# The first batch's attention: eight scalings of the second head on GpSimd, those of the last pair on ScalarE, and four copies of k on VectorE

## The chip, the cores and the metric

The kernel runs on one core of a Trainium2 chip. The metric is the device time of one execution in microseconds. A core has five engines that run their own instruction streams and meet through semaphores: TensorE (PE; its weight loads are PEld), VectorE (DVE), ScalarE (ACT), GpSimd (POOL) and SyncE (SP), which issues nearly all transfers here.

## The reference

The input is q, k and v in 4 batches of 8 heads, 768 positions of 64 channels. Attention with a window of 96 positions and 8 global ones and a linear distance bias is followed by a mixture of four two-layer networks over its output.

```python
scores = scale * np.matmul(q, k.transpose(0, 1, 3, 2)) + bias
scores = np.where(keep, scores, -1000000000.0)
a = np.exp(scores - np.max(scores, axis=-1, keepdims=True))
a = a / (np.sum(a, axis=-1, keepdims=True) + 1e-09)
x = np.matmul(a, v)
...
for e in range(E):
    h = np.maximum(x @ w1[e], 0.0)
    out += p[:, e:e + 1] * (h @ w2[e])
```

## The kernel before

The four batches' attention and networks share one program. Only the first batch's attention stands alone, at the start (`attention_early`); the other three run in small steps between the matmuls of the networks (`attention_chain`). All arithmetic here is in f32, and the networks' products in f32r parts.

**Tiles and steps.** The early attention goes over four pairs of heads, in the order `PAIRS = (0, 2, 1, 3)`; m is the place in that order, so the last pair is m = 3. Each pair has six tiles of 128 positions (t). I number a tile by n = 6m + t, 0 to 23, and the step that takes it up by the same number; two or three steps without a new tile follow. One call of `flow` is a step, and there four tiles are under way:

- the scores of tiles n and n+1 are multiplied on TensorE when n is even (`scores_early`, tile `ps`);
- in `softmax`, tile n-1 gets for each of its two heads j bias, sum and row minimum on VectorE (the `CUSTOM_DVE_ANT_0` rows) and the exponential with its row sum on ScalarE (`ACTIVATE pb<-pb,nmax` and a read of the accumulator);
- in the same call tile n-2 gets 1e-9 added to its sums (`zsum`), their reciprocal, and the scaling of its probabilities `pb` by it, head 0 and then head 1. All of that is on VectorE; the scalings are the rows `TENSOR_SCALAR_CACHE_REDUCE pb<-pb,zsum`;
- in `turn`, tile n-3 is transposed by TensorE into `pt` (the rows `pt<-ident,pb`, four transposes, each of which needs the scaled half that it turns), and ScalarE copies it to `pT`;
- once three tiles are turned, `weigh` multiplies them with v (`px`), and ScalarE copies that to `x`.

A tile with t = 0 has half as many columns.

**Preparing the next pair.** `AHEAD` says behind which steps a piece of `prepare_early` is called: q's first three tiles, k's first, k's second, q's second. TensorE transposes three tiles of 128x128 into a `pt` tile and ScalarE copies or scales them into `early_q` or `early_k` (128x384). Behind k's first half GpSimd spreads the global columns (`COPY early_k<-early_k`); ahead of k's second half `windows` starts a transfer `vg<-v` and a copy of it on GpSimd. Those of the pair m = 1 are at the steps 3 to 6 (k's halves at 4 and 5), of m = 2 at 7 to 10 (k's at 8 and 9), of m = 3 at 12 to 15 (k's at 13 and 14).

**GpSimd's other work in this part.** `biases` makes the distance biases of two heads at a time (`nbias`, two instructions of 128x384) behind the steps 3, 6 and 8. At the end of step 9 `load_plain(2)` starts the transfer of the network's first weights into `w1s`, and `load_w2` the next; at the end of step 11 GpSimd gets the four sums over those weights (`TENSOR_TENSOR w1s<-w1s`). From step 14 it splits `w2s`, from step 19 it makes the next unit's sums and `w1s`. VectorE gets four sums of the attention's output (`xB`, `first_sums(0)`) behind the steps 17 to 20.

**Order.** The wrapper `Ordered` is on through all of this: each instruction is tied behind the one written before it on its engine, so each engine's order is that of the program, and so is SyncE's order of transfers. Waits are for data and for free buffers: the transfer of v for m = 3, ahead of `w1s` in SyncE's queue, needs the buffer that m = 0's v leaves once tiles 3 to 5 are weighed.

Of the kernel before, what the change touches and what calls it, by code (L numbers as in the profile page):

```python
# [18 lines left out]
P = 128  # L19
# [167 lines left out]
def attn_moe_kernel(ctx: ExitStack, tc, q, k, v, n_global, n_local, domain_probs, w1, w2, out):  # L187
# [5 lines left out]
    NPAIR = H // 2  # L193
# [16 lines left out]
    ve, ac, po, sy, te = (Ordered(tc, e) for e in (nc.vector, nc.scalar, nc.gpsimd, nc.sync, nc.tensor))  # L210

    PAIRS = (0, 2, 1, 3)
# [2 lines left out]

    BIASES = ((0, 1), (0, 3), (1, 0), (1, 2))

    ONSTEPS = 6

    HELDSTEPS = 14  # L220
# [108 lines left out]
    def transpose_half(A, nat, hf):  # L329
        tp = A.pt.tile([P, 512], F32, name="pt")  # L330
        for t in range(TPH):
            te.transpose(tp[:, t * P : (t + 1) * P], nat[:, hf * TPH + t].rearrange("p j d -> p (j d)"), ident)
        return tp
# [30 lines left out]
        if hf == 0:  # L364
            ve.tensor_copy(kd[:, :, :, P:], f32(kd[:, :, 0:1, :NGLOB]).to_broadcast([P, 2, NQT, NGLOB]))

    def prepare_early(A, nat, hf, name, got):

        tp = transpose_half(A, nat, hf)
        tpv = tp[:, :HALF].rearrange("p (t c) -> p t c", c=P)  # L370
        pl = slice(hf * TPH, (hf + 1) * TPH)
        if name == "q":
            if hf == 0:
                got["q"] = A.qd.tile([P, NQT, P], F32, name="early_q")
            ac.activation(got["q"][:, pl, :], tpv, AF.Copy, scale=-SCALE)
            return
        if hf == 0:
            got["k"] = A.kd.tile([P, NQT, PL], F32, name="early_k")
        dst = got["k"]
        ac.copy(dst[:, pl, :P], tpv)  # L380
        if hf == 0:
            po.tensor_copy(dst[:, :, P:], dst[:, 0:1, :NGLOB].to_broadcast([P, NQT, NGLOB]))

    def windows(A, vt):

        vg = A.vg.tile([P, 2, NQT, D], F32, name="vg")
        sy.dma_start(vg[:NPREV], vt[NGLOB:])
        po.tensor_copy(vg[NPREV:], vt[:NGLOB, :, 0:1, :].to_broadcast([NGLOB, 2, NQT, D]))
        return vg
# [17 lines left out]
    def scores_early(A, t0, got):  # L407


        heads = [A.ps.tile([P, 2, 2 * P], F32, name=f"ps{j}") for j in range(2)]  # L410
        for t in (t0, t0 + 1):
            c0 = max(t - 1, 0) * PL + (0 if t == 0 else NGLOB)
            n = P if t == 0 else 2 * P
            for j in range(2):
                own = slice(j * D, (j + 1) * D)
                win = got["k"].rearrange("p t c -> p (t c)")[own, c0 : c0 + n]
                te.matmul(heads[j][:, t - t0, :n], got["q"][own, t, :], win, start=True, stop=True)
        return [[heads[j][:, i] for j in range(2)] for i in range(2)]

    def softmax(A, new, old):  # L420


        if old:
            pb, zsum = old["pb"], old["zsum"]
        if new:
            t, pr, ps = new["t"], new["pr"], new["ps"]
            cols = slice(0, P) if t == 0 else slice(0, 2 * P)
            bcol = slice(2 * P, 3 * P) if t == 0 else slice(0, 2 * P)
            new["pcol"] = pcol = slice(P, 2 * P) if t == 0 else slice(0, 2 * P)
            nmax = A.small.tile([P, 2], F32, name="nmax")  # L430
            new["zsum"] = A.small.tile([P, 2], F32, name="zsum")
            new["pb"] = A.pb.tile([P, 2, 2 * P], F32, name="pb")
        for j in range(2):
            if new:
                e = new["pb"][:, j, pcol]
                ve.tensor_tensor_reduce(
                    e, ps[j][:, cols], nbias[:, 2 * pr + j, bcol], 1.0, 3.0e38, ALU.add, ALU.min, nmax[:, j : j + 1]
                )
                ac.activation(
                    e, e, AF.Exp, bias=nmax[:, j : j + 1], scale=-1.0, accum_out=new["zsum"][:, j : j + 1]  # L440
                )
            if old:
                if j == 1:
                    ve.reciprocal(zsum, zsum)
                elif A.early:

                    old["spare"] = spare = A.small.tile([P, 3], F32, name="spare")
                    ve.tensor_scalar(zsum, zsum, 1e-9, None, op0=ALU.add, op1=ALU.add, accum_out=spare[:, 2:3])
                else:
                    ac.activation(zsum, zsum, AF.Copy, bias=1e-9)  # L450
        if old:
            for j in range(2):
                p = pb[:, j, old["pcol"]]
                if A.early:
                    ve.tensor_scalar(
                        p, p, zsum[:, j : j + 1], None, op0=ALU.mult, op1=ALU.add, accum_out=old["spare"][:, j : j + 1]
                    )
                else:
                    ac.activation(p, p, AF.Copy, scale=zsum[:, j : j + 1])

    def turn(A, tile_):

        t, pb = tile_["t"], tile_["pb"]
        pt = A.pt.tile([P, 2, 2, P], F32, name="pt")
        pT = A.pT.tile([P, 2, 2, P], F32, name="pT")
        w0 = 1 if t == 0 else 0
        for w in range(w0, 2):
            for j in range(2):
                te.transpose(pt[:, w, j, :], pb[:, j, w * P : (w + 1) * P], ident)
        ac.copy(pT[:, w0:], pt[:, w0:])  # L470
        tile_["pT"] = pT
# [27 lines left out]
    def attention_early(A):  # L499

        b = 0
        x = xs[b] = xp.tile([P, NPAIR, S], F32, name="x")
        tiles, turned, ahead = [None] * 4, [], [None]

        def flow(new=None):

            one, two, three, four = tiles
            if new:
                if new["t"] % 2 == 0:
                    new["ps"], ahead[0] = scores_early(A, new["t"], gots[new["pr"]])  # L510
                else:
                    new["ps"] = ahead[0]
            if four:
                turned.append(four)
            softmax(A, one, two)
            if three:
                turn(A, three)
            if len(turned) == TPH:
                weigh(A, turned, x, b)
                turned.clear()  # L520
            tiles[:] = [new, one, two, three]

        def start(pr):

            nats[pr] = {n: next(load(A, src, b, pr, n)) for n, src in (("q", q), ("k", k), ("v", v))}

        def prepare_all(pr):

            nat, got = nats[pr], gots[pr]
            got["v"] = nat  # L530
            prepare_early(A, nat["q"], 0, "q", got)
            if pr:
                yield 1
            prepare_early(A, nat["k"], 0, "k", got)
            yield 1
            nat["vg"] = windows(A, nat["v"])
            prepare_early(A, nat["k"], 1, "k", got)
            yield 1
            prepare_early(A, nat["q"], 1, "q", got)
            yield 1  # L540

        nats, gots = {}, [{} for _ in range(NPAIR)]
        halves = [load(A, src, b, 0, n, 2) for n, src in (("q", q), ("k", k))]
        bias = biases(start_stack.enter_context(tc.tile_pool(name="setup", bufs=1)))
        next(bias)
        nats[0] = dict(zip(("q", "k"), (next(h) for h in halves)))
        for h in halves:
            next(h)
        nats[0]["v"] = next(load(A, v, b, 0, "v"))
        todo = [prepare_all(pr) for pr in PAIRS]  # L550
        next(bias)
        next(todo[0])
        start(PAIRS[1])
        for m, pr in enumerate(PAIRS):
            cur = gots[pr]
            for t in range(NQT):
                if t == 2 and m + 2 < NPAIR:
                    start(PAIRS[m + 2])
                flow({"t": t, "pr": pr, **cur})
                if (m, t) in BIASES:  # L560
                    next(bias)
                for _ in range(AHEAD[m][t]):
                    while todo and next(todo[0], 0) == 0:
                        todo.pop(0)
                yield
        while any(tiles):
            flow()
            yield
# [401 lines left out]
    with ExitStack() as start_stack:  # L970
        A = Pools(start_stack, "start", st=1, kd=2, qd=2, nat=2, natv=3, pb=4, ps=2, pt=3, px=1, early=True)
# [15 lines left out]
    A = Pools(  # L987
        att_stack, "att", st=1, kd=1, qd=2, nat=1, natv=1, pb=2, ps=2, pt=2, px=0, early=False, side="right"
    )
# [373 lines left out]
    for b in range(LATE):  # L1363
# [9 lines left out]
        for n, (fn, i) in enumerate(events):  # L1373
# [15 lines left out]
            for _ in fn(i):  # L1389
                work_chores()  # L1390
                done += 1
                if b == 0 and done == ONSTEPS:
                    next(mix, None)
# [59 lines left out]
```

## Time and profile before

| | us |
|---|---|
| median of 3 runs | 1162.91 (1162.72 to 1163.08) |
| span of the profiled execution | 1162.9 |
| early attention, in the span | from the start to about 60 |
| networks and the other attentions | about 60 to the end |

The profiled execution's own time is its span, 1162.9 us; nothing lies around it that the times show. TensorE is busy 98% of the span, VectorE 73%, ScalarE 53%, GpSimd 52%. Times of the trace are microseconds from the span's start. In a row, the first number is the start, the second the length; a bracket gives the idle time before it and what ended it. Lengths of successive instructions on one engine overlap a little, so the distance from start to start is what one costs. The line L43 is the wrapper `Ordered`, so rows are told apart by their tiles.

### The profile page before, as it was taken

The page shows a single profiled execution, that of the slowest core. Times are in us where ns is not written, and L with a number is a line of the kernel's source. Part 1 is how long each engine was busy: PE and PEld are TensorE (multiplying, and loading weights), DVE is VectorE, ACT ScalarE, POOL GpSimd, SP SyncE. Part 2 cuts the span into 40 slices and gives each one's busy share as a digit, 9 for nine tenths or more (in the row PEclk, how much of TensorE's full clock was granted, in tenths as well). Part 3 has the DMA queues.
Part 4 walks back from the last instruction along what each step waited for, and adds up shares of the span by engine and source line. Part 5 has one row for each costly group of instructions (what it writes and reads, how often), then busy time and mean ns, then how long its engine had stood idle before and what let it go on. Part 6 is the DMA issues. An engine that isn't in the chain of part 4 may idle for free.

```text
span 1162.9 us, 21146 instructions
## 1 busy us (share of the span) xinstructions
PE 1140.5 (98%) x7474; PEld 1062.6 (91%) x7474; DVE 853.2 (73%) x1944; ACT 618.2 (53%) x1597; POOL 606.6 (52%) x592
## 2 busy tenths in 40 slices
PE   7899999999999999999999999999999999999997
PEld 5678898989888989899998899999999999999997
DVE  7977776767767777776776777777777777777776
ACT  6854767777653665655565334444445444444443
POOL 5676645554343314222222327777778855555554
PEclk9999999999999999999999999999999999999999
DMA  9558798778775889978868668888887687777764
GB/s 185 149 172 290 268 294 258 269 253 255 247 261 206 282 269 286 282 234 279 257 196 288 207 215 304 306 302 300 284 314 281 240 303 239 249 247 247 245 232 131
DMA packets 181744, 294.32 MB, mean 253 GB/s; under 512 B 86400, under 2 KB 137088, under 8 KB 169344
## 3 DMA queue, kind: packets, MB, share of 16 engines
q1 hardware_dynamic: 177600, 286.61, 75.0%
q10 hardware_dynamic: 4032, 6.30, 1.5%
q8 instruction: 61, 1.00, 0.4%
q14 instruction: 51, 0.42, 0.1%
HBM read 207.93 MB, written 70.78 MB: 240 GB/s over the span
## 4 chain that ended last, share of the span: by engine, by line
PE 87%; DVE 5%; ACT 3%; POOL 2%; DMA 1%; issue 1%; DVEq 0%; ACTq 0%; POOLq 0%
PE pm L43 36%; PE pf L43 19%; PE X L43 11%; PE Y L43 9%; PE pt L43 7%; PE ps L43 4%; ACT pb L43 1%; DVE pb L43 1%; POOL w1s L43 1%; PE px L43 1%; DVE acc L43 1%; DVE xB L43 1%; DMA x_last<-piece 0%; DVE hA L43 0%; DVE pm L43 0%
## 5 line engine op out<-in xcount | busy, mean ns | idle before, releaser
L43 PE MATMUL pm<-w2s,h 128*128 128x512 f32 x1152 | 282.8, 395 | 3.6 <-DVE h L43 2.6
L43 PEld LDWEIGHTS pm<-w2s,h 128*128 128x128 f32 x1152 | 210.7, 188 | 46.5 <-DVE h L43 4.5
L43 ACT ACTIVATE hf<-pf 128x384 f32<-128x384 f32 x128 | 62.8, 491 | 248.3 <-DVE pf L43 247.1
L43 POOL TENSOR_TENSOR hS<-sf,hS 128x384 fp32r<-128x384 f32 x126 | 134.3, 1084 | 113.0 <-ACT hS L43 112.2
L43 DVE SCALAR_TENSOR_TENSOR acc<-pm,prob,acc 128x512 f32<-128x512 f32 x180 | 132.4, 748 | 54.5 <-PE pm L43 53.6
L43 POOL TENSOR_TENSOR sums<-raw 128x256 f32<-128x256 f32 x54 | 39.2, 745 | 211.8 <-DMA raw<-in_moe_w_dram 133.4
L43 PE MATMUL pm<-xT,w1s 128*128 128x384 f32 x744 | 147.9, 341 | 0.0
L43 PE MATMUL pf<-xT,w1s 128*128 128x384 f32 x768 | 146.5, 335 | 0.9 <-ACT hf L43 0.7
L43 PEld LDWEIGHTS pf<-xT,w1s 128*128 128x128 f32 x768 | 131.4, 188 | 1.7 <-ACT hf L43 1.2
L43 PEld LDWEIGHTS pm<-xT,w1s 128*128 128x128 f32 x744 | 128.0, 188 | 0.7 <-issue 0.7
L43 ACT ACTIVATE pb<-pb,nmax 128x256 f32<-128x256 f32 (+1 forms) x192 | 94.2, 498 | 58.1 <-DVE nmax L43 54.2
L43 DVE TENSOR_TENSOR hA<-hf,hA 128x384 fp32r<-128x384 f32 x94 | 84.6, 925 | 50.6 <-ACT hA L43 49.1
L43 PE MATMUL pm<-xB,w1s 128*128 128x384 f32 x574 | 116.8, 344 | 0.1
L43 PE MATMUL pf<-xB,w1s 128*128 128x384 f32 x576 | 110.7, 335 | 0.2 <-ACT hf L43 0.2
L43 PEld LDWEIGHTS pm<-xB,w1s 128*128 128x128 f32 x574 | 99.9, 188 | 5.5 <-issue 1.4
L43 ACT ACTIVATE h<-pm 128x384 fp32r<-128x384 f32 x128 | 62.0, 490 | 74.4 <-DVE pm L43 73.3
L43 PEld LDWEIGHTS pf<-xB,w1s 128*128 128x128 f32 x576 | 98.7, 188 | 0.6 <-ACT hf L43 0.4
L43 POOL TENSOR_TENSOR sf<-hf 128x384 f32<-128x384 f32 x63 | 70.3, 1116 | 43.6 <-ACT hf L43 43.6
L43 DVE CUSTOM_DVE_ANT_0 pb<-ps,nbias 128x256 f32<-128x256 f32 (+1 forms) x192 | 72.3, 395 | 5.8 <-PE ps L43 4.8
L43 DVE SCALAR_TENSOR_TENSOR h<-pm,h 128x384 fp32r<-128x384 f32 x128 | 69.5, 550 | 8.4 <-ACT h L43 6.8
L43 PE MATMUL Y<-w2b,hS 128*128 128x256 f32 x576 | 74.0, 282 | 0.0
L43 PE MATMUL X<-w2b,hS 128*128 128x256 f32 x576 | 73.9, 282 | 0.0
(159 smaller groups left out, 2183.5 us busy)
## 6 DMA issues: line engine op xcount, KB each, us to landing
w1s<-kept SPq DMA_DIRECT2D x47, 1792.0 KB, 8.2
w2b<-kept SPq DMA_DIRECT2D x224, 256.0 KB, 4.3
kept<-w1s SPq DMA_DIRECT2D x16, 1792.0 KB, 7.3
raw<-in_moe_w_dram SPq DMA_DIRECT2D x43, 512.0 KB, 4.7
kept<-w2s SPq DMA_DIRECT2D x16, 1024.0 KB, 6.9
w2s<-kept SPq DMA_DIRECT2D x16, 1024.0 KB, 5.5
qd<-qd SPq DMA_DIRECT2D x48, 192.0 KB, 3.2
v<-in_v_dram SPq DMA_DIRECT2D x16, 384.0 KB, 4.1
```

The source lines that it names most:

```text
L43: ins = fn(*args, **kwargs)
```

## The change

The second head's scaling (j = 1) leaves VectorE for 14 of the 24 tiles. Eight, listed in `BY_POOL` as (m, t), go to GpSimd as `tensor_scalar_mul`: the tiles 2, 4, 5, 7, 9, 10, 11 and 12. All six of the last pair fall to the `else` branch and become activations on ScalarE. The accumulator's read behind each of the 14 scalings goes with them. ScalarE's four copies into `early_k` of the pairs m = 1 and m = 2 become copies on VectorE, at the same place of the program. No transfer is added or moved.

```diff
+    BY_POOL = ((0, 2), (0, 4), (0, 5), (1, 1), (1, 3), (1, 4), (1, 5), (2, 0))
...
-    def prepare_early(A, nat, hf, name, got):
+    def prepare_early(A, nat, hf, name, got, pr):
...
-        ac.copy(dst[:, pl, :P], tpv)
+        (ve.tensor_copy if pr in PAIRS[1:3] else ac.copy)(dst[:, pl, :P], tpv)
...
-                if A.early:
+                if A.early and j == 1 and (old["m"], old["t"]) in BY_POOL:
+                    po.tensor_scalar_mul(p, p, zsum[:, j : j + 1])
+                elif A.early and (j == 0 or old["m"] < NPAIR - 1):
                     ve.tensor_scalar(
                         p, p, zsum[:, j : j + 1], None, op0=ALU.mult, op1=ALU.add, accum_out=old["spare"][:, j : j + 1]
                     )
...
-                flow({"t": t, "pr": pr, **cur})
+                flow({"t": t, "pr": pr, "m": m, **cur})
```

The four calls of `prepare_early` pass `pr` on.

## Rows read from the trace of the kernel before

**Rows 1.** Stretches: length, busy time of PE, PEld, DVE, ACT, POOL, clock, DMA.

```profile
20.00:40.00 20.00, 19.89 (x198) 15.38 (x198) 18.34 (x119) 20.00 (x69) 11.04 (x14) 1.00 0.67 168
60.00:74.00 14.00, 12.70 (x42) 7.62 (x42) 11.75 (x24) 6.78 (x11) 8.55 (x7) 1.00 0.28 81
74.00:110.00 36.00, 35.88 (x194) 33.45 (x195) 26.57 (x48) 16.83 (x35) 30.77 (x30) 1.00 0.87 296
```

**Rows 2.** Timeline of ScalarE: start, us, engine, operation, idle before.

```profile
17.34 0.59 ACT L43 COPY pT<-pt 128x512 f32<-128x512 f32 x1 [0.65 <-PE pt L43]
17.82 0.48 ACT L43 COPY early_k<-pt 128x384 f32<-128x384 f32 x1
18.20 0.52 ACT L43 ACTIVATE pb<-pb,nmax 128x256 f32<-128x256 f32 x1
...
18.70 0.50 ACT L43 ACTIVATE pb<-pb,nmax 128x256 f32<-128x256 f32 x1
...
33.94 0.68 ACT L43 COPY pT<-pt 128x512 f32<-128x512 f32 x1
...
43.03 0.51 ACT L43 ACTIVATE pb<-pb,nmax 128x256 f32<-128x256 f32 x1 [1.27 <-DVE zsum L43]
...
52.99 0.51 ACT L43 ACTIVATE pb<-pb,nmax 128x256 f32<-128x256 f32 x1 [0.20 <-DVE zsum L43]
```

**Rows 3.** Timeline of VectorE over one step, and the next one's start.

```profile
15.13 0.42 DVE L43 CUSTOM_DVE_ANT_0 pb<-ps,nbias 128x256 f32<-128x256 f32 x1
...
15.90 0.16 DVE L43 RECIPROCAL zsum<-zsum 128x2 f32<-128x2 f32 x1
16.09 0.48 DVE L43 TENSOR_SCALAR_CACHE_REDUCE pb<-pb,zsum 128x256 f32<-128x256 f32 x1
...
16.50 0.47 DVE L43 TENSOR_SCALAR_CACHE_REDUCE pb<-pb,zsum 128x256 f32<-128x256 f32 x1
...
16.90 0.42 DVE L43 CUSTOM_DVE_ANT_0 pb<-ps,nbias 128x256 f32<-128x256 f32 x1
```

**Rows 4.** Timeline of TensorE.

```profile
17.14 0.49 PE L43 MATMUL pt<-ident,k 128*128 128x128 f32 x3
...
23.54 0.66 PE L43 MATMUL pt<-ident,pb 128*128 128x128 f32 x4
...
25.87 0.39 PE L43 MATMUL px<-pT,v 128*64 128x128 f32 x4
...
32.53 0.60 PE L43 MATMUL pt<-ident,pb 128*128 128x128 f32 x4
```

**Rows 5.** Timeline of GpSimd.

```profile
19.68 4.78 POOL L43 TENSOR_SCALAR nbias<-dist 128x384 bf16<-128x384 f32 x4
...
34.16 2.92 POOL L43 TENSOR_TENSOR w1s<-w1s 128x256 f32<-128x256 f32 x4 [7.04 <-DMA w1s<-in_moe_w_dram]
37.03 0.34 POOL L43 COPY early_k<-early_k 128x192 f32<-128x192 f32 x1
...
40.91 1.27 POOL L43 TENSOR_TENSOR w2s<-raw,w2s 128x512 fp32r<-128x512 f32 x1
```

**Rows 6.** Timeline of SyncE's queue.

```profile
27.50 0.58 SPq L43 DMA_DIRECT2D w1s<-in_moe_w_dram  x1
```

**Rows 7.** Groups by line and form on GpSimd: xcount | busy, mean ns.

```profile
L43 POOL TENSOR_SCALAR nbias<-dist 128x384 bf16<-128x384 f32 x6 | 7.0, 1177 | 1.0 <-DVE dist L43 0.7
...
L43 POOL TENSOR_SCALAR low<-rel 128x256 f32<-128x256 f32 x1 | 1.1, 1098 | 0.1
...
L43 POOL CAST w1s<-raw 128x256 fp32r<-128x256 f32 x1 | 0.4, 391 | 0.0
```

**Rows 8.** The same view on VectorE, an operation with a PSUM input.

```profile
L43 DVE TENSOR_TENSOR pm<-pm,vv 128x384 f32<-128x384 f32 x64 | 35.7, 558 | 4.4 <-PE pm L43 4.3
```

**Rows 9.** Timeline of VectorE: two of the four sums of x.

```profile
41.28 1.31 DVE L43 TENSOR_TENSOR xB<-x 128x384 f32<-128x384 f32 x1
...
48.47 0.55 DVE L43 TENSOR_TENSOR xB<-x,xB 128x384 f32<-128x384 f32 x1
```

More of the change, by code (lines that the diff above doesn't have):

```diff
@@ L530, in prepare_all @@
             got["v"] = nat
-            prepare_early(A, nat["q"], 0, "q", got)
+            prepare_early(A, nat["q"], 0, "q", got, pr)
             if pr:
                 yield 1
-            prepare_early(A, nat["k"], 0, "k", got)
+            prepare_early(A, nat["k"], 0, "k", got, pr)
             yield 1
             nat["vg"] = windows(A, nat["v"])
-            prepare_early(A, nat["k"], 1, "k", got)
+            prepare_early(A, nat["k"], 1, "k", got, pr)
             yield 1
-            prepare_early(A, nat["q"], 1, "q", got)
+            prepare_early(A, nat["q"], 1, "q", got, pr)
             yield 1
```

## The prediction

> **What bounds the kernel now.** I read the stretches first. Behind the first attention TensorE has no room: from 74 to 110 us it works 35.88 of 36 us, from 60 to 74 it still misses 1.3 [rows 1]. Whatever moves the end of the first attention therefore moves the end of the kernel, and little can take it up again: at most that 1.3. So the question is only when the first attention ends, near 60 us.
>
> There the timelines of the engines count. From 20 to 40 us ScalarE is busy without a gap (20.00 of 20) while TensorE shows 19.89 and VectorE 18.34 [rows 1]; three engines are close together, so each can be what others wait for. In the last pair it is VectorE: ScalarE waits 1.27 us at 43.03 and 0.20 at 52.99, both ended by VectorE [rows 2]. A plain step costs VectorE 1.77 (15.13 to 16.90): the reciprocal starts 0.77 into it, head 0's scaling 0.96, head 1's 1.37, and a scaling costs 0.41 from start to start [rows 3].
>
> GpSimd looks free in sums of busy time, and it is not when it matters. At 19.68 it runs four bias instructions, 4.78 us. Then it stands 7.04 us for the weights in `w1s` and makes their four sums from 34.16 to 37.08; the spreading of k's global columns, written behind them, starts at 37.03 [rows 5]. The weights' transfer is issued at 27.50 [rows 6], and SyncE comes to it behind v's transfer, which needs the buffer left when tiles 3 to 5 are weighed, at 25.87 + 0.39 = 26.26 [rows 4].
>
> **The change part by part.**
>
> *Work removed.* VectorE loses 14 scalings: 8 to GpSimd (seven at 0.41, the half tile 12 less), 6 to ScalarE. ScalarE loses four copies at 0.38 (17.82 to 18.20), 1.5 in all [rows 2]. Taken alone this would be worth up to 1.5 us where ScalarE is full. It is the price of the waits that decides.
>
> *A copy of k on VectorE.* No such copy stands in the trace. The nearest row with a PSUM input of 128x384 is a sum, 558 ns [rows 8]; a scaling of 0.48 costs 0.41 from start to start [rows 3], so I take 0.5, between 0.41 (a scaling of fewer columns) and 0.56. The copy also waits: in step 4 VectorE would be free at 16.50, with head 1 gone to GpSimd, but TensorE's transposes of k run from 17.14 to 17.63 [rows 3, 4]. VectorE idles 1.1 us, copies to 18.13, and only then starts step 5, which began at 16.90. Queued behind the copy are the minima, so ScalarE's exponentials too. Step 5 has both scalings of tile 3 (1.77, to 19.90) and k's second copy (to 20.40). Step 6 starts there; tile 4's scaling is free for GpSimd at 20.40 + 0.96 = 21.36.
>
> *A scaling on GpSimd.* The trace has none of 128x256 by one operand per partition. A plain cast of that form takes 0.391, a two-operation one 1.098; the one-operation bias product takes 1.177 for 384 columns [rows 7], and two thirds of it are 0.79. I take 0.85, nearest to that row plus some start. [...]
>
> *First stall.* GpSimd takes tile 4 from 21.36 to 22.21. Next in its order stand the two bias products of step 6, half of the 4.78 [rows 5]: to 24.60. Only then tile 5: to 25.45. TensorE transposed tile 5 at 23.54 [rows 4]. It stands there 1.9 us later than before, and with it k's transposes of the pair m = 2, the weighing of tiles 3 to 5 and, through the buffer, the transfer of `w1s`. Bounds by the scaling's price: at 0.391 1.0 us late, at 1.098 2.4; nothing, if GpSimd gets tile 4 at the old time and is quick.
>
> *Second stall.* Tiles 10, 11 and 12 are written for steps 12 to 14, behind the four sums of step 11. Their start follows the weighing of tiles 3 to 5 by 34.16 - 26.26 = 7.90, nearly all of it transfer, and that distance stays, since the same transfers are issued in the same order from the same event. So the sums start at 26.26 + 1.9 + 7.9 = 36.1, end 2.92 later at 39.0, and tile 10 is scaled at 39.8. TensorE transposed tile 10 at 32.53 [rows 4, 5]. It stands there, 7.3 us behind, with the next pair's k and scores queued behind it. Tiles 11 and 12 then follow on GpSimd in 0.85 and less, ahead of TensorE. VectorE and ScalarE can run about a step ahead and stop.
>
> *What is given back.* ScalarE copied tile 10's transposes at 33.94, 0.8 after they ended at 32.53 + 0.60 [rows 2, 4]; TensorE's delay eats this slack first: 7.3 - 0.8 = 6.5 reach ScalarE. The first sum of x took 1.31 beside a GpSimd product that began at 40.91, another 0.55 [rows 5, 9]; late by 6 us, it meets GpSimd waiting for the next weights, and 0.75 come back. It might meet other work as before; then nothing does.
>
> *Last pair.* VectorE's step falls from 1.77 to 1.36. ScalarE's was two exponentials at 0.50 and a copy at 0.48 (17.34 to 17.82) [rows 2], 1.48; an activation of the same form adds at most 0.50 (an exponential's whole price) and at least 0.41 (VectorE's): 1.89 to 1.98, over VectorE's old 1.77. ScalarE takes the place of VectorE as the bound. In the first two such steps VectorE's earlier start (0.27 and 0.41) can be worth 0.7; the five full ones lose up to 5 x 0.21 = 1.0. I take 0.3 lost. That the engine relieved was the bound of this stretch gains nothing, since the work goes to the next in line.
>
> *The sum.* + 6.5 - 0.75 + 0.3 = 6.1 us later at the end of the attention. The measured execution's span, 1162.9, is the median's 1162.91; so 1169.0 us. Own range: the scaling at 0.391 takes 0.9 from the first stall and 0.5 from the second (1167.6), at 1.098 adds 0.75 (1169.8); no first stall at all leaves 1167.1; with the last pair's 0.7 gained, 1166.1; without the 0.75 and with 1.0 lost in the last pair on top of 1169.8, 1171.2. That is 1166.1 to 1171.2.
>
> **The rivals.**
>
> *GpSimd is in time, and it gets faster.* This needs the sums done before tile 10 is due: TensorE at 32.53, less 0.85 and 2.92, so weights landed by 28.8, 1.3 us after the issue that in the trace takes 6.7 to the sums [rows 4 to 6]. Or GpSimd would have to pass over waiting sums; the row at 37.03, which starts only when the last sum is through, speaks against it. If it held, ScalarE's 1.5 us of copies would be saved where it is full, and the 0.7 of the last pair's first steps: 1160.7.
> [...]
>
> *The stall is small.* The weights land sooner than they did, as TensorE's delay leaves the transfer queues emptier. If the sums do not wait at all, GpSimd gets to them when tile 9 is scaled, one step of VectorE (1.77) before tile 10 is due. Their 2.92 then leave 1.15, and the slower scaling 0.44 more. With the first stall that is 1.9 + 1.6 - 0.8 - 0.75 + 0.3 = 2.3: 1165.2. For it speaks that v, `vg`, two weights share the queues; against it that all four are still issued together.
>
> *The delay is taken up later.* The 1.3 us that TensorE misses from 60 to 74 and slack in the weights' splits would have to hold it; 6 us do not fit into that [rows 1]. If it were so, 1163.
>
> **How the numbers follow.** A difference of 0.2%, 2.3 us, is about what a measurement of this kernel can tell from none: 1160.6 to 1165.2. The forecast with both waits gets 0.70, the small stall 0.13 (at 1165.2 half of it within 0.2%), no visible change 0.08, the gain 0.09 (at 1160.7 half of it within 0.2%). So slower 0.70 + 0.06 = 0.76, same 0.07 + 0.08 + 0.04 = 0.19, faster 0.05. The likeliest case lies at 1166.1 to 1171.2; reaching into the small stall, 1164.6 to 1171.5 leaves out 2 in 10.
>
> **What would show it.** On GpSimd the first bias product of the second group starts behind a scaling, and tile 5's scaling behind two of them; four sums of `w1s` near 36 us, then two scalings in a row. On TensorE a wait of over 4 us ended by GpSimd ahead of one transpose group, near 35 to 40 us, and a shorter one near 24. On VectorE a wait for TensorE ahead of each of the four copies. In the last pair ScalarE without gaps. Attention ends near 66 instead of 60, and TensorE's stretches after it look as they did. The forecast is wrong if a scaling of tile 10 runs ahead of the sums, if the weights land well before 35, or if the GpSimd scaling costs over 1.1 us or under 0.4.

## The result and the profile after

The change makes the kernel slower: 1175.14 us in the median of 4 runs (1173.39 to 1176.82) beside 1162.99 (1162.72 to 1165.34) for the kernel before on the same chip. The ratio is 1.0096, with an interval of 1.0078 to 1.0114, which is 11.2 us of 1163; the two medians differ by 12.2. Two later measurements of the same kernel gave 1.0073 and 1.0083 (below); the mean of the three is 1.0084, 9.8 us. The forecast was 1169.0, with 1171.5 as its upper end: the sign held, the size was too small.

The profiled execution took 1176.82 us for a span of 1175.0. So 1.8 us lie outside the span here, and 1.7 to 1.9 in every later run that lists both. That the profiled execution of before took just its span, as told ahead of the prediction, is therefore doubtful. The forecast's difference of 6.1 doesn't depend on it.

The place of the loss is the one foreseen. ScalarE's last copy of the attention's output came at 59.98 before; after, the timeline of ScalarE has

```profile
41.32 0.59 ACT L43 COPY pT<-pt 128x512 f32<-128x512 f32 x1 [4.18 <-PE pt L43]
...
73.25 0.48 ACT L43 COPY x<-px 128x384 f32<-128x384 f32 x1 [0.89 <-PE px L43]
```

The first row answers to 33.94 in [rows 2]: tile 10's transposes are copied 7.4 us later, and the attention ends 13.3 later. The spans differ by 12.1, so all but 1.2 of it reaches the end. The question is the step from 7.4 to 13.3.

GpSimd's timeline after, beside [rows 5]:

```profile
21.82 0.92 POOL L43 TENSOR_SCALAR pb<-pb,zsum 128x256 f32<-128x256 f32 x1 [1.97 <-ACT pb L43]
22.71 2.40 POOL L43 TENSOR_SCALAR nbias<-dist 128x384 bf16<-128x384 f32 x2
25.21 0.92 POOL L43 TENSOR_SCALAR pb<-pb,zsum 128x256 f32<-128x256 f32 x1
26.10 2.30 POOL L43 TENSOR_SCALAR nbias<-dist 128x384 bf16<-128x384 f32 x2
...
36.49 2.89 POOL L43 TENSOR_TENSOR w1s<-w1s 128x256 f32<-128x256 f32 x4 [2.95 <-DMA w1s<-in_moe_w_dram]
39.36 1.82 POOL L43 TENSOR_SCALAR pb<-pb,zsum 128x256 f32<-128x256 f32 x2
```

Tile 4's scaling, two bias products, tile 5's scaling; later the four sums, and behind them the tiles 10 and 11 in one go. TensorE's timeline, beside [rows 4]:

```profile
24.66 0.33 PE L43 MATMUL pt<-ident,pb 128*128 128x128 f32 x1
26.19 0.55 PE L43 MATMUL pt<-ident,pb 128*128 128x128 f32 x3 [1.19 <-POOL pb L43]
...
35.69 0.27 PE L43 MATMUL pt<-ident,pb 128*128 128x128 f32 x1
40.33 0.90 PE L43 MATMUL pt<-ident,pb 128*128 128x128 f32 x3 [4.37 <-POOL pb L43]
41.02 0.85 PE L43 MATMUL pt<-ident,k 128*128 128x128 f32 x3
41.80 2.08 PE L43 MATMUL ps<-early_k,early_q 64*128 64x256 f32 x8
...
58.98 0.98 PE L43 MATMUL pt<-ident,pb 128*128 128x128 f32 x2 [2.17 <-DVE pb L43]
...
62.65 2.08 PE L43 MATMUL ps<-early_k,early_q 64*128 64x256 f32 x8
```

Both stalls stand where they were forecast, ended by GpSimd. What was not forecast stands behind them: three transposes of k take 0.85 instead of 0.49 [rows 4], and eight score products 2.08, where the same eight took 1.14 in the steps in between. The windows of the kernel after show the clock that goes with it (columns as in [rows 1]; the figure ahead of the DMA share, third from the end, is the granted clock):

```profile
36.00:38.00 2.00, 0.00 (x0) 0.00 (x0) 0.79 (x6) 1.15 (x5) 1.43 (x3) 0.96 0.07 28
38.00:44.00 6.00, 3.67 (x15) 2.52 (x16) 0.15 (x2) 2.05 (x6) 4.10 (x7) 0.50 0.01 3
44.00:46.00 2.00, 2.00 (x21) 1.83 (x22) 1.94 (x12) 1.04 (x3) 0.00 (x0) 0.83 0.00 0
58.00:60.00 2.00, 0.96 (x4) 0.47 (x6) 1.96 (x13) 1.86 (x6) 1.92 (x3) 0.58 0.15 18
60.00:64.00 4.00, 4.00 (x30) 3.50 (x32) 2.30 (x16) 2.98 (x10) 3.84 (x5) 0.50 0.97 345
64.00:66.00 2.00, 1.98 (x12) 1.09 (x9) 1.21 (x8) 1.05 (x4) 0.58 (x1) 0.71 0.22 86
74.00:88.00 14.00, 13.10 (x45) 7.92 (x45) 12.24 (x25) 6.33 (x10) 9.28 (x8) 1.00 0.34 105
88.00:120.00 32.00, 32.00 (x173) 29.79 (x172) 22.81 (x39) 16.83 (x34) 29.97 (x29) 1.00 0.89 308
```

While TensorE stands idle for tile 10, its granted clock goes from 1.00 to 0.50 (0.96 in 36 to 38 us, 0.50 in 38 to 44) and stays there until about 45 us (0.83 in 44 to 46), although TensorE is at work from 40.33 on. A second low stretch begins between 58 and 60 (0.58 there, 0.50 in 60 to 64), after waits of 1.18, 0.54 and 2.17 us for VectorE with work between them. Before, each of these windows up to 66 us shows 1.00. The first fall came in a wait of 4.37 us, the second without so long a wait. The last two rows answer to the last two of [rows 1] and look alike: behind the attention nothing is taken up, as forecast.

VectorE's timeline after, the first copies of k of each pair and the four sums of x, and GpSimd's instruction that runs when each sum begins:

```profile
18.00 0.56 DVE L43 COPY early_k<-pt 128x384 f32<-128x384 f32 x1 [1.35 <-PE pt L43]
...
27.10 0.56 DVE L43 COPY early_k<-pt 128x384 f32<-128x384 f32 x1 [1.52 <-PE pt L43]
...
50.38 1.60 DVE L43 TENSOR_TENSOR xB<-x 128x384 f32<-128x384 f32 x1
...
53.65 1.05 DVE L43 TENSOR_TENSOR xB<-xB,x 128x384 f32<-128x384 f32 x1
...
56.12 1.49 DVE L43 TENSOR_TENSOR xB<-x,xB 128x384 f32<-128x384 f32 x1
...
58.75 0.89 DVE L43 TENSOR_TENSOR xB<-x,xB 128x384 f32<-128x384 f32 x1
```
```profile
50.29 1.27 POOL L43 TENSOR_TENSOR w2s<-raw,w2s 128x512 fp32r<-128x512 f32 x1
...
53.57 0.73 POOL L43 TENSOR_TENSOR sums<-raw 128x256 f32<-128x256 f32 x1
...
55.93 1.27 POOL L43 TENSOR_TENSOR w1s<-raw,w1s 128x512 fp32r<-128x512 f32 x1
...
58.61 0.61 POOL L43 CAST w1s<-sums 128x512 fp32r<-128x512 f32 x1
```

The four sums take 5.03 together. Before they took 1.31, 0.55, 0.83 and 0.55, together 3.24 [rows 9 for the first and last]. The forecast had the first fall to 0.55; they grew by 1.8. Each of the four begins while GpSimd's instruction runs and ends 0.40 to 0.42 behind its end (51.98 beside 51.56, 54.70 beside 54.30, 57.61 beside 57.20, 59.64 beside 59.22). Before, the first did the same: it ended at 42.59, GpSimd's product at 42.18 [rows 5, 9].

### The profile page after: what moved, and what is told of

Its sections match the earlier page's. It is cut to its first block, busy times and chain, and to the rows that moved or that the text cites. A ratio compares the mean times of both kernels' runs of the same rounds, so it can differ in the third digit from the quotient of the medians.

```text
span 1175.0 us, 21127 instructions
## 1 busy us (share of the span) xinstructions
PE 1145.9 (98%) x7474; PEld 1066.1 (91%) x7474; DVE 852.0 (73%) x1920; ACT 620.1 (53%) x1599; POOL 613.3 (52%) x600
## 4 chain that ended last, share of the span: by engine, by line
PE 90%; DVE 5%; ACT 2%; POOL 1%; issue 1%; DMA 1%; DVEq 0%; ACTq 0%; POOLq 0%
PE pm L43 39%; PE pf L43 19%; PE X L43 11%; PE Y L43 9%; PE pt L43 7%; PE ps L43 4%; DVE pb L43 1%; PE px L43 1%; ACT pb L43 1%; DVE xB L43 1%; POOL w1s L43 1%; DVE hA L43 0%; DMA out_dram<-acc 0%; DVE acc L43 0%; POOL xB L43 0%
```

## The experiments

Theory: the loss is the order of GpSimd's queue, which makes TensorE wait, and the low clock that follows its waits. Rivals: VectorE's copies of k, ScalarE's added work in the last pair, or GpSimd's added load as such. Each diff is against the kernel after. A ratio is to the kernel before on the same chip, medians of which were 1164.4 to 1164.9 us; an interval is of 95%. The expectations count their totals from 1162.9, about 2 us below these medians.

The profiles differ in their start. In those of before, after, e1_kcopy, e3_pool, e4_sums_late, e13_filled_all and e16_first_filled_more eight score products at 14.5 to 14.6 take 2.08 us; in the other ten they begin at 14.0 to 14.4 and take 1.13 or 1.14. With the early start the whole change turned tile 10 1.6 us earlier. So a last copy shows a mechanism, and prices are taken from the times.

### One part of the change alone

e1_kcopy keeps only the copies on VectorE:

```diff
-    BY_POOL = ((0, 2), (0, 4), (0, 5), (1, 1), (1, 3), (1, 4), (1, 5), (2, 0))
+    BY_POOL = ()
...
-                elif A.early and (j == 0 or old["m"] < NPAIR - 1):
+                elif A.early:
```

> Only the four copies of k go to VectorE; every scaling stays there. Theory of order: VectorE waits 1 to 1.5 us for TensorE's transposes ahead of the first copies of each pair, but nothing stands behind GpSimd; ScalarE gets 1.5 us back. Attention's last copy to x (59.98 in the kernel before, 73.25 in the changed one) at 60.5 to 62, the clock at its upper level, total 1163.5 to 1165. Rival (the copies are what costs most of the 12 us): last copy behind 65, total over 1168. Second rival (the copies relieve ScalarE as meant): 58.5, total 1161.5.

Measured: 1.0008 [0.9999, 1.0018]; last copy to x at 62.17, 0.2 over its range. Both rivals lie outside the interval.

e2_last keeps only the last pair's scalings on ScalarE:

```diff
-    BY_POOL = ((0, 2), (0, 4), (0, 5), (1, 1), (1, 3), (1, 4), (1, 5), (2, 0))
+    BY_POOL = ()
...
-        (ve.tensor_copy if pr in PAIRS[1:3] else ac.copy)(dst[:, pl, :P], tpv)
+        ac.copy(dst[:, pl, :P], tpv)
```

> Only the last pair's second head is scaled on ScalarE. Theory: ScalarE takes VectorE's place as the bound of those steps, last copy to x at 59.8 to 60.6, total 1162.7 to 1163.6. Rival (VectorE's relief is worth its 2.3 us): last copy near 58, total 1160.7.

Measured: 0.9999 [0.9989, 1.0009]; last copy at 60.13, as the theory said. In this profile ScalarE's steps of the last pair follow each other without a gap from 49.05 on and take 1.86 (52.93 to 54.79), where before they took 1.76 with a gap of 0.20 (52.99 to 54.75):

```profile
52.06 0.50 ACT L43 ACTIVATE pb<-pb,zsum 128x256 f32<-128x256 f32 x1
...
52.93 0.52 ACT L43 ACTIVATE pb<-pb,nmax 128x256 f32<-128x256 f32 x1
...
54.79 0.52 ACT L43 ACTIVATE pb<-pb,nmax 128x256 f32<-128x256 f32 x1
```

e3_pool keeps only the eight scalings on GpSimd (the second hunk of e1_kcopy and the second of e2_last):

> Only the eight scalings go to GpSimd. Theory of order: tile 5 waits behind two bias products (TensorE 0.5 to 1 us late near 24 us), tile 10 behind the four sums over w1s (TensorE idle some 5 us from about 33), and the clock falls to its lower level behind that idle time: last copy to x at 68 to 72, total 1170 to 1174, that is three quarters or more of the whole loss. Rival (the loss comes from the copies of k and the last pair as much as from GpSimd): total below 1168.

Measured: 1.0067 [1.0050, 1.0083]; last copy at 66.84, ahead of the range of 68 to 72. TensorE's longest wait for GpSimd is 4.5 us. So most of the loss, 7.8 of 9.8 us, comes with the eight scalings; the two other parts alone come to +0.9 and -0.1 us, and the interval of each includes 0.

### The order of GpSimd's queue

e4_sums_late is the whole change, with the four sums over `w1s` written six steps behind its transfer instead of two; the transfer stays where it was:

```diff
-                chores += [load_plain(2), load_w2(0, lead=5, eng=po)]
+                chores += [load_plain(6), load_w2(0, lead=5, eng=po)]
```

> The whole change, but GpSimd's four sums over w1s are written four steps later, behind the scaling of tile 12; the transfer starts as before. Theory of order: no wait of TensorE for GpSimd near 36 to 40 us, the granted clock stays up there, what is left is the first stall (2.5) and the last pair: last copy to x at 62 to 65, total 1165 to 1168. Rival (GpSimd's scalings are slow wherever they stand, or the clock falls for another reason): last copy behind 69, total over 1171.

Measured: 1.0024 [1.0013, 1.0034]; last copy at 64.12. The scalings of tiles 9 to 11 and the sums on GpSimd's timeline:

```profile
32.65 0.92 POOL L43 TENSOR_SCALAR pb<-pb,zsum 128x256 f32<-128x256 f32 x1 [2.12 <-ACT pb L43]
33.98 0.92 POOL L43 TENSOR_SCALAR pb<-pb,zsum 128x256 f32<-128x256 f32 x1 [0.41 <-DVE zsum L43]
35.30 0.92 POOL L43 TENSOR_SCALAR pb<-pb,zsum 128x256 f32<-128x256 f32 x1 [0.39 <-DVE zsum L43]
...
43.60 3.26 POOL L43 TENSOR_TENSOR w1s<-w1s 128x256 f32<-128x256 f32 x4
```

Tile 10 is now scaled at 33.98 instead of 39.36, and the sums no longer wait for their weights. From the mean 1.0084 to 1.0024 is 7.0 us: the second stall with all that follows it.

e8_order also moves the bias products of step 6 to step 7 and those of step 8 to step 14:

```diff
-    BIASES = ((0, 1), (0, 3), (1, 0), (1, 2))
+    BIASES = ((0, 1), (0, 3), (1, 1), (2, 2))
...
-                chores += [load_plain(2), load_w2(0, lead=5, eng=po)]
+                chores += [load_plain(6), load_w2(0, lead=5, eng=po)]
```

> The whole change with GpSimd's order mended at both places: the sums over w1s four steps later, and the two pairs of bias products one and six steps later, so that none stands ahead of a scaling that is due. Theory: no wait of TensorE for GpSimd at all; what is left are VectorE's waits for k's transposes and the last pair; last copy to x at 61.5 to 63.5, total 1164 to 1166.5. Rival (GpSimd's scaling is itself too slow for its place): waits for GpSimd of 0.5 us and more remain, total over 1167.

Measured: 1.0008 [0.9999, 1.0018]; last copy at 61.80; TensorE's longest wait for GpSimd is 0.3 us. The first stall is worth the difference to e4_sums_late, 0.0016 or 1.9 us.

e9_pool_order has that order and the eight scalings alone (e8_order with the hunks of e3_pool):

> Only the eight scalings on GpSimd, with its order mended as in the run before; k's copies and the last pair as they were. Theory: VectorE's relief of 3 us buys nothing, since ScalarE is full where it comes: last copy to x at 59 to 60.5, total 1162 to 1164, the same as the kernel before. Rival (VectorE's relief shortens the first attention): 57.5 to 58.5, total near 1161.

Measured: 1.0000 [0.9991, 1.0010]; last copy at 59.87. Moving the scalings costs nothing once nothing stands ahead of them in GpSimd's queue, and brings nothing that an interval of 1 us to either side can show. This profile is ahead of before by 0.47 us at tile 10's turn (32.06 beside 32.53), but that is its early start: e2_last, where VectorE works as before up to there, starts early too and turns tile 10 at 32.11. The difference to e8_order, 0.0008 or 0.9 us, is that of the copies of k and the last pair; e1_kcopy gives the same 0.9 for the copies alone. Each is at the edge of its interval.

### TensorE kept busy through its waits

Here the whole change stays, and transposes of the identity into a spare buffer, whose result nobody reads, stand ahead of the turns of some tiles:

```diff
+                for i in range({(1, 4): 36}.get((three["m"], three["t"]), 0)):
+                    if i == 0:
+                        spare = A.pt.tile([P, 512], F32, name="pt")
+                    te.transpose(spare[:, i % 4 * P : (i % 4 + 1) * P], ident, ident)
```

That is e6_filled, 36 ahead of tile 10. e7_filled_both adds 8 ahead of tile 16's turn, (2, 4), and 16 ahead of tile 18's, (3, 0); e13_filled_all also 7 each at (3, 2) and (3, 3).

> The whole change, and 36 transposes of the identity into a PSUM tile that nobody reads, ahead of tile 10's transposes: TensorE works through most of the 4.4 us in which it stood. Theory of the clock: the granted clock stays at its upper level from 38 to 45 us, k's transposes, scores and transposes after the wait take 2.0 us again and not 3.7, and the attention's last copy to x moves from 73.25 to 70 to 72, total 1171.5 to 1174. Rival (the clock falls for another reason, such as the whole core's load): the clock row shows 0.5 again there and the total stays at 1175.

Measured: 1.0069 [1.0052, 1.0085]; last copy at 68.76, ahead of its range. The clock stays at 1.00 until 56, as the theory said, and is 0.51 in 56 to 58 and 0.64 in 58 to 60 us.

> As the run before, with 8 such transposes ahead of tile 16's and 16 ahead of tile 18's, where TensorE waited for VectorE from 52 to 59 us. Theory of the clock: no stretch below the upper level between 36 and 66 us, last copy to x at 68 to 70, total 1169.5 to 1172.5: what the clock cost is 3 to 5 us of the 12. Rival (the second low stretch comes of other causes): 0.5 again near 59 to 64.

Measured: 1.0063 [1.0047, 1.0080]; last copy at 68.00; the clock is 1.00 until 60, then 0.70 and, in 62 to 64, 0.50. The theory wanted no low stretch up to 66; the fall only moved.

> The whole change, with transposes of the identity into a spare buffer ahead of tile 10's turn (36), tile 16's (8), tile 18's (16) and tiles 20's and 21's (7 each), so that TensorE does not stand idle in its waits for GpSimd, ScalarE and VectorE. Theory (the low clock is worth 3 to 5 us of the 11): granted clock 1.00 from 36 to 66 us, last copy to x at 66.5 to 68.5 us, ratio 1.0050 to 1.0065, with e12_after_again at 1.008 to 1.011. Rival (the clock costs little, since TensorE waits anyway): ratio within 0.001 of that of e12_after_again.

Measured: 1.0064 [1.0049, 1.0078]; last copy at 67.55; no window from 30 to 68 us shows less than 1.00. TensorE's timeline around tile 10 and one window:

```profile
35.70 4.09 PE L43 MATMUL pt<-ident 128*128 128x128 f32 x36
39.63 0.27 PE L43 MATMUL pt<-ident,pb 128*128 128x128 f32 x1
40.11 0.55 PE L43 MATMUL pt<-ident,pb 128*128 128x128 f32 x3 [0.20 <-POOL pb L43]
40.49 0.49 PE L43 MATMUL pt<-ident,k 128*128 128x128 f32 x3
40.91 1.14 PE L43 MATMUL ps<-early_k,early_q 64*128 64x256 f32 x8
```
```profile
38.00:40.00 2.00, 1.91 (x18) 1.67 (x16) 0.17 (x2) 0.00 (x0) 2.00 (x3) 1.00 0.00 0
```

Tile 10 comes no earlier than in the kernel after (40.11 beside 40.33), the work behind it runs at the old rate. From that turn to the last copy of x it is 67.55 - 40.11 = 27.44 us; before it was 59.98 - 32.53 = 27.45 [rows 4], after 73.25 - 40.33 = 32.92.

The whole change once more, on the same chip as e13_filled_all:

> The whole change once more, nothing else, to stand on the same chip as e13_filled_all. Theory (clock falls after the wait for the tenth tile and again in the last pair): ratio 1.008 to 1.011, granted clock near 0.5 over 38 to 44 us and again for 3 to 6 us after 56. Rival (the low clock of the first profile was an accident of that execution): clock 1.00 in one of the two stretches or both, and a ratio of 1.005 to 1.007.

Measured: 1.0073 [1.0058, 1.0087]; the clock is 0.50 in 40 to 42 and in 58 to 60, with shorter low stretches than in the first profile; last copy at 69.34. Expected was 1.008 to 1.011, and e13_filled_all is only 0.0009, 1.0 us, below it, which is what that run's rival (the clock costs little) named. So the whole change and two of the filled kernels were measured again side by side:

> The whole change, nothing else, in five rounds beside the two filled kernels. Theory (after the stalls' 7.5 us come 1 to 4 more from the low clock, in most executions): ratio 1.008 to 1.010, and above that of e15_filled_more by more than the two intervals. Rival (the clock falls in the profiled execution, but what it costs is mostly hidden behind VectorE and GpSimd): ratio 1.006 to 1.0075, inside the interval of e15_filled_more.

> The kernel of e13_filled_all (the whole change with transposes of the identity ahead of the turns of tiles 10, 16, 18, 20 and 21) in five rounds. Theory: granted clock 1.00 from 36 to 66 us and ratio 1.0060 to 1.0068, the 7.5 us that the turn of tile 10 comes late and nothing behind it. Rival: the same ratio as e14_after_more.

> The kernel of e6_filled (the whole change with 36 transposes of the identity ahead of tile 10's turn alone) in five rounds. Theory (each of the two low stretches costs its own part): between the two others, 1.0065 to 1.0080. Rival (the clock's cost is hidden): the same ratio as e14_after_more.

Measured: 1.0083 [1.0069, 1.0097], 1.0058 [1.0044, 1.0071] and 1.0076 [1.0063, 1.0090], in this order, medians 1174.19, 1170.92 and 1173.61 us; the second lies just under the 1.0060 expected. Windows of e14_after_more and of e15_filled_more:

```profile
38.00:44.00 6.00, 5.22 (x22) 4.07 (x23) 1.50 (x10) 2.59 (x7) 2.54 (x4) 0.52 0.01 3
...
58.00:62.00 4.00, 4.00 (x33) 3.01 (x32) 2.81 (x19) 3.64 (x13) 3.76 (x6) 0.59 0.41 117
```
```profile
38.00:44.00 6.00, 4.90 (x52) 3.79 (x51) 2.25 (x13) 3.88 (x13) 3.32 (x6) 1.00 0.00 0
...
58.00:62.00 4.00, 4.00 (x38) 3.24 (x33) 3.24 (x22) 4.00 (x16) 3.50 (x4) 1.00 0.90 342
```

So the low clock costs 2.9 us by these ratios (3.3 by the medians) and 1.0 by the pair before, and with the clock held the change still costs 6.8 (0.0058) and 7.5 (0.0064). The middle kernel lies between, as the theory said, but nearer to the unfilled one, whose interval holds it, and its clock falls later instead, to 0.50 in 62 to 64. The two outer intervals overlap by 0.0002, where the theory wanted them apart: the order of the three supports it, the exact size is loose.

The profiles give the mechanism more clearly. From tile 10's turn to the last copy, which leaves the start out, the whole change needs 32.92, 30.57 and 31.79 us in its three profiles; with some waits filled it is 29.93 (e6_filled), 29.48 (e7_filled_both) and 29.05 (e16_first_filled_more), with all of them filled 27.44 and 28.71, and before 27.45. Not all of this reaches the end: from the last copy on, the spans have 1101.8 to 1102.2 us left in the whole change and 1103.0 and 1103.4 in the two filled ones. Why is not known.

### Versions meant to beat both

e10_deferred takes the order of e8_order (the sums four steps later), gives each copy of k to VectorE one step later (so that VectorE need not wait for TensorE's transposes), returns the last pair to VectorE and adds a few transposes of the identity:

```diff
+        def finish(copy):
+            copy(dst[:, pl, :P], tpv)
...
+        if pr in PAIRS[1:3]:
+            owed.append(finish)
...
+                while owed:
+                    owed.pop(0)(ve.tensor_copy)
```

> The eight scalings on GpSimd and k's copies on VectorE, but the sums of w1 are asked for two pairs later, two of the four bias products go to a later pair, each copy of k's transposes is given to VectorE one step later, the last pair's scaling is on VectorE as before, and some transposes of the identity into a spare buffer stand ahead of the turns of tiles 16 and 18. Theory (stalls behind GpSimd's queue and behind VectorE's copies, and the clock after them, are the whole loss): with no tile late the 1.5 us that ScalarE no longer spends on k's copies can show: last copy to x at 57.5 to 59.5 us (59.98 before), ratio 0.998 to 1.000. Rival (ScalarE is not what sets the pace in the first attention, so its relief is worth nothing, and GpSimd's added work slows VectorE): last copy at 60 to 62 us, ratio 1.000 to 1.0015.

Measured: 1.0034 [1.0021, 1.0046]; last copy at 62.54. It misses both its numbers and the rival's. Its waits of TensorE name a new one:

```profile
PE ps L43 <- DVE early_k L43: 0.8, 1, 0.8
```

The scores now wait for k, and the clock is 0.50 in 56 to 58 in spite of the added transposes. ScalarE's relief shows nowhere.

e11_pool_filled is e9_pool_order with the same added transposes, 4 at (2, 4) and 12 at (3, 0):

> The eight scalings alone, in the mended order of GpSimd's queue (the run e9_pool_order), with the same added transposes of the identity ahead of the turns of tiles 16 and 18. Theory (in e9_pool_order the turn of tile 18 came 0.8 us earlier than before, and this was given back to the low clock that followed TensorE's wait at 48 us): granted clock 1.00 all through 46 to 54 us, last copy to x at 58.7 to 59.3 us, ratio 0.9990 to 0.9997. Rival (the lead of 0.8 us is lost to VectorE's or ScalarE's own pace in the last two pairs whatever the clock): last copy at 59.7 to 60.5 us, ratio 0.9997 to 1.001.

Measured: 1.0017 [1.0009, 1.0026]; last copy at 59.75, with the clock at 1.00 in every window from 30 to 68 us. The lead of 0.8 us is lost whatever the clock, as the rival said; the ratio lies above both ranges. That it is slower than e9_pool_order is not settled: its attention ends as early, and in its profile the next loss is at 98.58, where GpSimd waits 3.51 us for weights, where before it waited 1.99 at 97.22. One execution doesn't show whether the added transposes are to blame.

No version beat the kernel before; e9_pool_order and e2_last equal it.

## Why the prediction was right in sign and too small

**What bounds the kernel, and that nothing is taken up later: right.** Of the 13.3 us at the last copy 12.1 reach the end.

**A copy of k on VectorE: right.** It took 0.56 (0.5 was taken, 0.56 the bound), VectorE waited 1.35 and 1.52 ahead of the first copy of each pair (1.1 forecast). The sign named a wait ahead of each of the four; the second copies had none and 0.24. All four together are worth about 0.9 us (e1_kcopy, -0.1 to 2.1).

**A scaling on GpSimd: nearly right.** 0.92 instead of 0.85. The row of the bias products was the right neighbour. On VectorE the same form takes 0.48 [rows 3].

**First stall: right in place.** Tile 5 was scaled until 26.13 (25.45 forecast), TensorE went on at 26.19, 2.65 us later than its turn before [rows 4] (1.9 forecast). Only 1.19 of that is its wait for GpSimd; it came to the turn 1.1 late already (24.66 beside 23.54). Taken away the stall is worth 1.9 us of the time (e4_sums_late to e8_order).

**Second stall: right to half a microsecond.** The sums began at 36.49 (36.1), tile 10 was scaled at 40.28, which is 39.36 + 0.92 (39.8), and TensorE went on at 40.33.

**What is given back, and the sum: this step failed.** It let TensorE go on at its old rate behind the stall, which put the clock at nothing without a reason, and it took 0.8 of slack and 0.75 of the first sum of x off. Its 6.1 us stand beside 9.8.

The larger miss is the clock. Without filler work the granted clock halves around the wait for tile 10 in each of the three profiles of the whole change (0.50 in 40 to 42 us in all of them), and again in the last pair (0.50 in 60 to 64, 58 to 60 and 60 to 62). That term, 1.0 and 2.9 us in two comparisons side by side, was missing, and no rival had it. The first stretch alone can be read off: the two halves of k for the pair m = 3 are transposed at 41.02 and 44.71, 3.69 apart; in e13_filled_all at 40.49 and 42.47, 1.98 apart. That is 1.7.

With the clock held the change costs 6.8 and 7.5 us (1.0058, 1.0064), nearer to 6.1 but above it. In e13_filled_all tile 10's turn is 7.58 late (40.11), ScalarE's copy of it 6.81 (40.75 beside 33.94), the last copy 7.57. So the 0.8 of slack was eaten as forecast, and behind it 0.76 were lost again, where the sum had -0.75 and +0.3.

The -0.75 had the wrong sign. GpSimd's own queue had slipped along with the attention, so it did not stand waiting when the sums of x came: the first sum met the same product over `w2s`, at 40.91 before [rows 5] and at 50.29 after. In after, e14_after_more, e15_filled_more and e13_filled_all the four sums take 5.03, 4.23, 4.97 and 3.71, before 3.24; none comes near four times 0.55. In the kernel after each of the four lasts as long as the rest of the GpSimd instruction that it runs into plus 0.40 to 0.42, so its length there depends on where GpSimd stands. What ties the two together no run shows. e15_filled_more needs 28.71 us from tile 10's turn (39.45) to the last copy (68.16), 1.27 more than e13_filled_all, with sums longer by 1.26.

**Last pair: right in its mechanism.** ScalarE takes VectorE's place as the bound: a step of 1.86 in e2_last (1.89 to 1.98 forecast). +0.3 was forecast and -0.1 measured [-1.3, +1.0], which does not tell the sign. In the whole change itself ScalarE had gaps there, against the sign named: it waited for TensorE, 1.00 at 62.77 and 0.94 at 65.58.

**The rivals.** "GpSimd is in time" failed as forecast in the change, and e9_pool_order and e8_order show that it would have gained nothing even then: the 1.5 us of ScalarE's copies and the 0.7 of the last pair did not appear, with TensorE's longest wait for GpSimd down to 0.3. That a full ScalarE from 20 to 40 us [rows 1] means a gain from relieving it was wrong. What bounds that stretch then is open: in e8_order no engine is full there (TensorE 19.28, ScalarE 19.10, VectorE 16.48 of 20 us). "The stall is small" and "taken up later" failed.

**The account** of the 9.8 us in one direction: the sums ahead of tiles 10 to 12, 7.0; the bias products ahead of tile 5, 1.9; the copies of k, 0.9; the scalings themselves and the last pair, 0. In the other: 6.8 to 7.5 with the clock held, the remaining 2 to 3 by the clock. Each term is a difference of ratios that are uncertain by about 0.001 (1.2 us). From 40 to 60 us the granted clock is 0.91 in the mean in the profiles of e1_kcopy, e4_sums_late, e8_order and e9_pool_order too, where before it is 1.00, so the small terms may hold some of the clock's cost as well.

## What to carry to other kernels

When work moves to an engine with free time, write down what stands ahead of each moved instruction in that engine's order, and until when: here an engine that was half free made its customers wait 4.4 us, and moving two kinds of work in its queue mended nearly all of it. Add to a forecast stall of TensorE what a lower clock behind it can cost: here the granted clock was 0.50 from 38 to 44 us around a wait of 4.37 us, which came to 1.7 us, and 1.00 with transposes in the wait. Do not count work taken off a full engine as time gained: here eight scalings off VectorE (1.0000) and, with them, four copies off ScalarE (1.0008) gained nothing.

## What the runs showed of the hardware

The granted clock did not come back when TensorE's work did: in the kernel after it was 0.50 from 38 to 44 us with TensorE working from 40.33 on, and 1.00 again from 46. Waits of about the same length had two outcomes here: TensorE stands for VectorE ahead of tile 18's turn 1.51 us before, where the clock is 1.00 in every window from 36 to 66 us, and 1.5 us in e9_pool_order, where it then falls to 0.50 in 49 to 52 us. In e13_filled_all, with 36 transposes (4.09 us) in the wait for tile 10, it stayed at 1.00. The same kernel's low stretches differ from one execution to the next: the last copy of x came at 73.25, 69.34 and 70.57 in its three profiles. Part of that is the start: eight score products at 14.63 take 2.08 us in the kernel after, and at 14.06 they take 1.13 in e12_after_again, where tile 10 is turned 1.6 us earlier (38.77 beside 40.33). Before's own profile has the late start (14.56, 2.08 us). The clock's column shows 1.00 in 14 to 16 us before and after, and 1.00 for 0 to 20 us in e12_after_again.

In the kernel after, each sum of two tiles of 128x384 on VectorE that begins during an instruction of GpSimd ends 0.40 to 0.42 us behind it, whether that has two inputs or is a cast. Before, the second sum, which began just ahead of GpSimd's, at 44.27, took 0.55, and GpSimd's sum over `raw`, from 44.30, took 1.11 instead of 0.72. With GpSimd idle such a sum took 0.56 (before, at 60.49).
